# Linear attention and a three-product feed-forward layer on one core: w_phi loaded from ScalarE's queue, the last tile's output in two halves, a new order

## The chip, the core and the metric

The kernel runs on one core of a Trainium2 chip. The core has a matrix engine (TensorE, PE in the profile; its weight loads are shown apart as PEld), a vector engine (VectorE, DVE), a scalar engine (ScalarE, ACT), GpSimd (POOL), and an engine that here only issues transfers (SyncE, SP). Each engine works through its own queue in order and waits there for what the others write. The metric is the device time of one execution in microseconds; lower is better.

## What is computed

q, k and v have 8 batches, 8 heads, 576 tokens and 64 columns. Both stages are in float32.

```
phi(x): p = x @ w_phi (64x128); p -= max|p| per token; [exp(p), exp(-p)]
kv  = phi(k)^T v,  z = sum over tokens of phi(k)
att = (phi(q) kv) / (phi(q) z + 1e-6)          # tokens x 512, all heads side by side
h   = att @ w_in (512x1024);  solu = h * softmax(h)
out = layernorm(solu) * g_ln @ w_out (1024x512)   # 4608 x 512
```

## The kernel before

**Attention.** The work is cut into 16 units, two to a batch. A unit has four heads, handled as two sub-steps ("sub" 0 and 1) of two heads. For each unit SP loads keys in three groups (a group 0 of 512 columns, a small one 1, a group 2 of 512; function `k_load`, L483), values, and queries. TensorE multiplies keys by w_phi (tile `wph`, results `pjk`), VectorE takes the maximum and subtracts it, ScalarE makes both exponentials. The first three units treat their queries in the same way (`q2_load`, L650, and results `pjq`); the later ones transpose them on VectorE and multiply by a split copy of w_phi (`w_hh`, `w_l`).

Each sub-step has one **visit** (`visit`, L580): TensorE multiplies the previous sub-step's query features by its kv matrix (`num`), then builds the present kv matrix (`kvT`), then the denominators (`den`). A visit needs the sums of the key features that GpSimd makes (`z_half`, L570, is the last of them). VectorE evicts the kv matrix, SP writes it to memory (`dk<-kvs`) and reads it back in another layout by four loads (`kvf<-dk`); the next visit needs them. This is called a turn below. The denominators go from ScalarE through VectorE, which takes the reciprocal (`cmr`), to a store by SP (`d<-cmr`) and come back spread over the partitions (`rb<-d`); GpSimd multiplies by them (`divide`, L828, tiles `xa` and `xb`).

**Feed-forward.** The 4608 tokens are 36 tiles of 128, numbered 0 to 35. float32 products are made of three products of split operands (high by high, high by low, low by high). For a tile ScalarE copies the high part of the input (`mxh`), GpSimd makes the low part (`mxl`), TensorE makes `h` in two half steps of 12 products, VectorE and ScalarE make solu (`eu`) and its statistics. Tiles 0 to 32 are turned by VectorE and a way through memory (`du<-ub`, four loads `uTs<-du`), split by ScalarE (`uhs`) and GpSimd (`uls`); tiles 33 to 35 are turned on TensorE (`uT`) and split by ScalarE and VectorE (`uh`, `ul`). Then `moe_o` (L1152) makes the output in two half steps of 12 products of 512 columns in one bank, `moe_oe` (L1162) evicts it on ScalarE with the scale (`os<-o,sc`), `moe_od` (L1166) stores it from SP's queue.

The weights w_in and w_out come as float64 in eight loads of 1 MB (`wraw`) at the start; ScalarE, VectorE and GpSimd turn them into float32 and split them (`win_h`, `win_l`, `w_out_h`, `w_out_l`), beside the first units of attention.

**What sets the order.** Every step is one entry of a list of operations, made by `op(...)` with an engine, a cost, and the steps and buffers that it needs. The table `SEQUENCE` (L50) names the number of every entry; `Plan.order` (L232) walks through it, gives each buffer to the next that asks for it, and each engine gets its steps in that order. So the table fixes the order on every engine, and which of a tag's buffers a step takes: there are three for the large key and query loads (tag `rk`, L42), two banks `mo`, and for the last tiles two banks `tmo` (L47). A load into a buffer waits on SP until the previous contents have been read, and what is queued behind it on SP waits too.

w_phi is loaded twice, into two corners of `wph`, by `phi_load` (L353); VectorE clears the tile first.

Of the kernel before, what the change touches and what calls it, by code (L numbers as in the profile page):

```python
# [50 lines left out]
    88, 99, 0, 3, 2, 136, 126, 132, 102, 7, 89, 90, 100, 103, 198, 104, 199, 127, 107, 95, 108, 91, 101, 96,  # L51
    130, 8, 131, 14, 92, 133, 230, 105, 128, 97, 186, 137, 197, 134, 93, 129, 35, 98, 145, 224, 135, 94, 142,
    138, 106, 148, 9, 109, 149, 143, 139, 144, 118, 140, 234, 146, 150, 41, 10, 15, 187, 114, 11, 141, 151, 119,
    110, 164, 147, 165, 16, 120, 188, 121, 115, 153, 111, 152, 200, 205, 17, 112, 53, 231, 166, 154, 116, 201,
    36, 193, 232, 189, 156, 4, 233, 117, 167, 202, 155, 194, 169, 113, 37, 203, 225, 18, 158, 168, 157, 122,
    204, 190, 195, 28, 295, 38, 196, 6, 42, 226, 39, 12, 191, 228, 13, 170, 192, 235, 227, 171, 229, 172, 240,
    123, 159, 173, 241, 243, 236, 160, 216, 245, 47, 43, 54, 238, 44, 244, 174, 242, 175, 161, 55, 29, 296, 45,
    162, 246, 217, 328, 124, 30, 247, 249, 284, 248, 207, 56, 251, 250, 125, 218, 40, 208, 176, 31, 219, 48,
    209, 32, 177, 178, 179, 210, 49, 163, 252, 180, 212, 46, 237, 213, 254, 50, 214, 253, 255, 215, 51, 211,
    329, 256, 239, 436, 297, 206, 21, 386, 52, 303, 332, 304, 271, 57, 397, 262, 268, 285, 263, 59, 286, 269,  # L60
    333, 60, 58, 220, 633, 437, 330, 291, 273, 61, 264, 287, 270, 22, 331, 292, 272, 298, 221, 257, 438, 293,
    62, 299, 258, 288, 294, 387, 300, 289, 181, 344, 63, 265, 5, 182, 222, 23, 301, 305, 290, 259, 67, 302, 260,
    76, 314, 338, 79, 183, 73, 334, 184, 85, 64, 261, 306, 315, 310, 316, 398, 307, 311, 24, 317, 223, 267, 345,
    266, 346, 68, 19, 33, 65, 274, 20, 308, 275, 276, 309, 34, 335, 278, 277, 347, 279, 439, 349, 339, 348, 336,
    280, 312, 440, 318, 337, 388, 185, 313, 340, 319, 25, 350, 320, 321, 66, 351, 281, 74, 282, 389, 26, 341,
    352, 390, 75, 393, 391, 353, 27, 394, 441, 355, 442, 354, 372, 342, 373, 356, 77, 322, 374, 283, 70, 323,
    468, 358, 366, 1871, 357, 82, 367, 359, 324, 368, 343, 445, 360, 375, 1913, 1872, 443, 69, 395, 1873, 444,
    86, 361, 80, 1914, 446, 362, 377, 447, 550, 469, 614, 81, 405, 392, 1874, 399, 376, 406, 87, 396, 325, 83,
    326, 470, 363, 400, 1875, 448, 327, 369, 401, 511, 1876, 449, 416, 402, 407, 370, 1877, 371, 471, 408, 78,
    1915, 412, 450, 413, 417, 409, 472, 1880, 451, 477, 452, 473, 403, 475, 84, 404, 1916, 474, 410, 1881, 476,  # L70
    501, 551, 418, 478, 479, 453, 422, 1917, 1882, 500, 1883, 378, 552, 853, 1918, 1884, 1885, 379, 512, 1919,
    1892, 364, 411, 71, 1893, 419, 480, 380, 1894, 1886, 1922, 1923, 481, 423, 454, 424, 414, 482, 457, 455, 72,
    381, 458, 555, 553, 483, 1887, 1924, 425, 1895, 554, 484, 459, 1878, 1925, 415, 426, 456, 427, 556, 428,
    1920, 420, 559, 1926, 557, 1888, 1927, 558, 1896, 421, 560, 1897, 365, 429, 1928, 1898, 485, 460, 1901, 461,
    1934, 561, 1929, 486, 582, 1902, 583, 430, 1935, 502, 1903, 462, 382, 463, 520, 1930, 489, 584, 431, 503,
    664, 1904, 507, 519, 504, 505, 1921, 514, 432, 562, 506, 1936, 513, 563, 508, 490, 383, 564, 515, 509, 530,
    433, 516, 491, 1905, 517, 434, 565, 585, 435, 566, 587, 487, 567, 586, 1937, 464, 588, 488, 384, 510, 1906,
    518, 531, 568, 589, 1938, 591, 1931, 696, 590, 532, 1939, 571, 592, 665, 1879, 1940, 536, 572, 385, 1943,
    1932, 593, 1944, 666, 492, 573, 493, 1907, 1945, 1908, 1946, 521, 1947, 494, 697, 1948, 465, 594, 1889, 595,
    569, 615, 522, 596, 570, 698, 526, 523, 537, 524, 667, 538, 525, 597, 1909, 668, 626, 1949, 495, 1933, 533,  # L80
    975, 527, 1890, 625, 528, 466, 529, 496, 1950, 699, 539, 598, 671, 700, 1910, 540, 541, 542, 534, 497, 669,
    627, 673, 670, 498, 1951, 672, 535, 674, 1899, 467, 675, 543, 499, 1941, 574, 1955, 1956, 2018, 599, 1957,
    576, 575, 600, 603, 544, 676, 545, 1958, 677, 577, 778, 678, 2019, 546, 679, 740, 616, 1959, 680, 729, 681,
    547, 628, 617, 1960, 548, 1952, 618, 549, 604, 1961, 619, 620, 621, 601, 644, 622, 2020, 629, 623, 630, 624,
    1964, 1976, 645, 602, 1965, 703, 605, 701, 578, 705, 631, 2021, 810, 682, 632, 646, 702, 704, 706, 1900,
    650, 2022, 1942, 685, 2023, 779, 2024, 606, 683, 2027, 1966, 1967, 1968, 579, 1969, 580, 728, 607, 707,
# [1182 lines left out]
```

## Time and profile before

| | us |
|---|---|
| median of 3 runs | 719.25 (719.08 to 719.99) |
| the profiled execution | 717.91 |
| its span, first to last instruction | 716.1 |
| TensorE busy | 694.4 (97% of the span) |
| GpSimd busy | 513.7 |
| VectorE busy | 483.5 |
| ScalarE busy | 368.7 |

The granted clock of TensorE was 0.997 in the mean. The profile is of one execution, so its times lie within its own 717.91 us, which is 1.34 us less than the median. Matmuls are pipelined, so a row's length is longer than the distance to the next row; distances are taken from the starts. Nearly every row has the line L263, that of the helper through which all instructions go, so rows are told apart by their tiles: `out<-in`.

### The profile page before, as it was taken

The numbers are of one execution on the slowest core, as the hardware profiler recorded it, in microseconds if no ns is written. First come the engines' busy times: TensorE is split into PE (matmuls) and PEld (weight loads), VectorE is DVE, ScalarE is ACT, GpSimd is POOL, SyncE is SP. The second block draws the span as 40 slices with busy tenths as digits, with TensorE's granted clock in tenths as the row PEclk, the third lists the DMA queues.
The fourth block names the chain that finished last, engine by engine and source line by source line (L and its number), as shares of the span: only waits on it lengthen the run. The fifth ranks groups of instructions, "written<-read, shape, count | busy, mean of one in ns | idle before, by whom it ended". The sixth has DMA issues, their size and how long they took to land.

```text
span 716.1 us, 13369 instructions
## 1 busy us (share of the span) xinstructions
PE 694.4 (97%) x4858; PEld 517.8 (72%) x4858; DVE 483.5 (68%) x795; ACT 368.7 (51%) x683; POOL 513.7 (72%) x501
## 2 busy tenths in 40 slices
PE   6999889999999999999999999999999999999997
PEld 5656567777777777777776777777787777788886
DVE  5999878656867678478566688676687574544422
ACT  4888645644753555546555555545544554324221
POOL 1136999996889878887978987986877777445151
PEclk9999999999999999999999999999999999999999
DMA  7784365644763565637357367745664443512331
GB/s 258 286 274 103 79 181 167 189 136 118 199 189 121 159 194 159 199 106 205 111 161 183 118 179 185 192 133 139 177 182 119 144 135 77 155 56 72 125 102 75
DMA packets 113649, 109.96 MB, mean 154 GB/s; under 512 B 57648, under 2 KB 90928, under 8 KB 113072
## 3 DMA queue, kind: packets, MB, share of 16 engines
q1 hardware_dynamic: 113584, 109.11, 52.7%
q8 instruction: 39, 0.64, 0.4%
q14 instruction: 26, 0.21, 0.1%
HBM read 76.68 MB, written 32.39 MB: 152 GB/s over the span
## 4 chain that ended last, share of the span: by engine, by line
PE 81%; DVE 6%; DMA 5%; SPq 2%; ACT 2%; issue 2%; POOL 2%; POOLq 0%; ACTq 0%
PE o L263 26%; PE h L263 24%; PE kvT L263 9%; PE num L263 8%; PE pjk L263 5%; PE den L263 4%; PE pq L263 3%; DVE w L263 2%; SPq L263 2%; DMA kvf<-dk 2%; DVE m L263 1%; DMA dk<-kvs 1%; POOL xa L263 1%; DMA rawk<-in_k 1%; DMA rb<-d 1%
## 5 line engine op out<-in xcount | busy, mean ns | idle before, releaser
L263 ACT ACTIVATE ek<-dk 128x512 f32<-128x512 f32 (+1 forms) x160 | 86.5, 584 | 50.7 <-DVE dk L263 49.0
L263 PE MATMUL o<-w_out_h,uhs 128*128 128x512 f32 x264 | 106.5, 403 | 0.0
L263 PE MATMUL o<-w_out_h,uls 128*128 128x512 f32 x264 | 104.2, 395 | 0.0
L263 PE MATMUL o<-w_out_l,uhs 128*128 128x512 f32 x264 | 104.1, 394 | 0.0
L263 POOL TENSOR_TENSOR uls<-uTs,uhs 128x1024 fp32r<-128x1024 f32 x33 | 79.1, 2396 | 27.6 <-ACT uhs L263 21.1
L263 PE MATMUL h<-win_h,mxh 128*128 128x512 f32 x288 | 93.1, 404 | 0.1
L263 PE MATMUL h<-win_l,mxh 128*128 128x512 f32 x288 | 89.4, 392 | 0.0
L263 PE MATMUL h<-win_h,mxl 128*128 128x512 f32 x288 | 89.4, 391 | 0.0
L263 DVE TENSOR_REDUCE nm<-h 128x1 f32<-128x1024 f32 x36 | 43.8, 1217 | 60.1 <-PE h L263 60.0
L263 POOL TENSOR_TENSOR zt<-ek 128x512 f32<-128x512 f32 x52 | 67.2, 1293 | 16.8 <-ACT ek L263 15.2
L263 POOL TENSOR_TENSOR hq<-rawq,hq 64x1152 fp32r<-64x1152 f32 x26 | 69.0, 2655 | 9.6 <-issue 6.1
L263 PE MATMUL num<-fq,kvf 128*64 128x288 f32 x512 | 69.2, 412 | 2.9 <-DMA kvf<-dk 2.1
L263 ACT ACTIVATE fq<-pT 128x576 f32<-128x576 f32 x104 | 68.1, 678 | 7.4 <-DVE pT L263 7.4
L263 ACT ACTIVATE eu<-h,nm 128x1024 f32<-128x1024 f32 x36 | 40.1, 1115 | 53.2 <-DVE nm L263 47.6
L263 PEld LDWEIGHTS h<-win_l,mxh 128*128 128x128 f32 x288 | 54.0, 188 | 12.1
L263 PEld LDWEIGHTS h<-win_h,mxl 128*128 128x128 f32 x288 | 54.1, 188 | 12.1
L263 DVE TENSOR_TENSOR eu<-h,eu 128x1024 f32<-128x1024 f32 x36 | 43.8, 1217 | 27.4 <-ACT eu L263 27.3
L263 PE MATMUL kvT<-ek,rawv 128*64 128x256 f32 x512 | 61.1, 380 | 0.0
L263 DVE TENSOR_REDUCE m<-pjk 128x4 f32<-128x512 f32 (+1 forms) x80 | 48.4, 621 | 18.3 <-PE pjk L263 18.2
L263 DVE STREAM_TRANSPOSE blk<-pq 128x288 f32<-128x288 f32 x104 | 45.4, 457 | 22.0 <-PE pq L263 17.8
L263 PEld LDWEIGHTS h<-win_h,mxh 128*128 128x128 f32 x288 | 50.8, 189 | 10.9 <-issue 1.4
L263 PEld LDWEIGHTS num<-fq,kvf 128*64 128x64 f32 x512 | 34.5, 136 | 32.7 <-issue 10.2
(107 smaller groups left out, 1444.4 us busy)
## 6 DMA issues: line engine op xcount, KB each, us to landing
du<-ub SPq DMA_DIRECT2D x33, 512.0 KB, 2.8
uTs<-du SPq DMA_DIRECT2D x132, 128.0 KB, 3.4
rawq<-in_q SPq DMA_DIRECT2D x26, 576.0 KB, 4.5
rb<-d SPq DMA_DIRECT2D x64, 144.0 KB, 3.6
out<-os SPq DMA_DIRECT2D x36, 256.0 KB, 3.1
rawk<-in_k SPq DMA_DIRECT2D x32, 256.0 KB, 3.8
rawv<-in_v SPq DMA_DIRECT2D x32, 256.0 KB, 4.0
dk<-kvs SPq DMA_DIRECT2D x28, 192.0 KB, 2.3
```

The lines of the kernel that those rows point to most:

```text
L263: return self.tc.keep_in_program_order(method(*args, **kwargs))
```

## The change

Three things change. `phi_load` issues its two transfers from ScalarE's queue instead of SP's. For tile 35 the output is computed in two halves of 256 columns, each in a bank of its own (the first in a `tmo`, the second in an `mo` bank), all 24 products of a half before the next half; each half is evicted and stored by itself. The table `SEQUENCE` is replaced; its numbers from tile 35 on name other entries as well, since there is one more eviction and one more store.

```diff
@@ SEQUENCE = (
-    88, 99, 0, 3, 2, 136, 126, 132, 102, 7, 89, 90, 100, 103, 198, 104, 199, 127, 107, 95, 108, 91, 101, 96,
...
     def phi_load(j):
-        nc.sync.dma_start(out=wph[j * D : (j + 1) * D, j * F : (j + 1) * F], in_=w_phi)
+        nc.scalar.dma_start(out=wph[j * D : (j + 1) * D, j * F : (j + 1) * F], in_=w_phi)
...
-        op(("wp", j), "sync", dma(4 * D * F, True), -40 + j, phi_load, (j,))
+        op(("wp", j), "scalar", 600, -40 + j, phi_load, (j,))
...
+    LAST = NTOK // P - 1
+
+    def moe_o_last(t, half, tag):
+
+        uh, ul = M["uh", t], M["ul", t]
+        o = M["o", t, half] = bank(tag, [P, DM], "o")
+        cs = slice(half * 256, half * 256 + 256)
+        for fc in range(8):
+            for x, w in ((uh, "h"), (uh, "l"), (ul, "h")):
+                nc.tensor.matmul(
+                    o[:, :256], lhsT=x[:, fc, :], rhs=w_out_part(w, fc)[:, cs],
+                    start=(fc == 0 and x is uh and w == "h"), stop=(fc == 7 and x is ul),
+                )
+
+    def moe_oe_last(t, half):
+        if half == 0:
+            M["os", t] = sb("m2k", [P, DM], name="os")
+        nc.scalar.activation(
+            out=M["os", t][:, half * 256 : half * 256 + 256], in_=M["o", t, half][:, :256], func=AF.Copy, scale=M["sc", t]
+        )
+
+    def moe_od_last(t, half):
+        cs = slice(half * 256, half * 256 + 256)
+        nc.sync.dma_start(out=out[t * P : (t + 1) * P, cs], in_=M["os", t][:, cs])
...
+        for hf in range(2 if t == LAST else 0):
+            tg = ("tmo", "mo")[hf]
+            op(n("o", hf), "tensor", 24 * mm(256), z + 13 + 3 * hf, moe_o_last, (t, hf, tg),
+               [n("ul", i) for i in range(2)] + ([n("o", 0)] if hf else []), [(tg, n("o", hf))], [n("uh"), n("ul"), n("o", hf)])
...
+        if t == LAST:
+            continue
```

The new table keeps the rough order: a step of TensorE moves by about one place in the mean, one of SP by seven. Three places are shown, each before and now.

SP, at the start. `rawk` are keys, `rawq` queries of unit 0 (before, `rawq_108` is its first group, `rawq_110` the second and small one, `rawq_106` the third; now they are `rawq_106`, `rawq_110` and `rawq_147`), `rawv` and `vz` values, `wraw` 1 MB of weights. Before:

```order
L263 DMA rawk<-in_k 128x512
L263 DMA rawk<-in_k 128x128
L263 DMA wph<-in_w_phi 64x128 x2
L263 DMA rawq_106<-in_q 128x512
L263 DMA rawq_108<-in_q 128x512
L263 DMA rawq_110<-in_q 128x128
L263 DMA wraw_114<-in_w_in 128x2048
L263 DMA rawv<-in_v 128x512
L263 DMA vz_74<-in_v 64x128
L263 DMA vz_76<-in_v 64x128 x2
L263 DMA rawk<-in_k 128x512
```

Now, in the same place:

```order
L264 DMA rawk<-in_k 128x128
L264 DMA rawk<-in_k 128x512
L264 DMA rawq_106<-in_q 128x512
L264 DMA rawk<-in_k 128x512
L264 DMA rawq_110<-in_q 128x128
L264 DMA vz_74<-in_v 64x128
L264 DMA wraw_113<-in_w_in 128x2048
L264 DMA rawv<-in_v 128x512
L264 DMA rawk<-in_k 128x128
L264 DMA rawq_147<-in_q 128x512
L264 DMA wraw_151<-in_w_in 128x2048
```

The w_phi loads are gone from SP (they stand first on ScalarE now). Unit 0's third key group is the fourth load instead of the last row shown before, and it takes the third `rk` buffer; its third query group, before ahead of the weights in a buffer of its own, is now behind a 1 MB load and takes the buffer of the first key group.

SP, some 60 to 95 us in, around the load of unit 3's last key group, `rawk_1187` before and `rawk_901` now; `cmr` is the reciprocal denominator that VectorE makes, `d1` its store. Before:

```order
L263 DMA rawq_1104<-in_q 128x1152
L263 DMA kvf_1127<-dk_1102 32x12x32
L263 DMA d1_1174<-cmr_1168 128x9
L263 DMA rawq_1179<-in_q 128x1152
L263 DMA rawk_1183<-in_k 128x512
L263 DMA rawk_1187<-in_k 128x512
L263 DMA vz1_76<-in_v 64x128
L263 DMA rawv_1204<-in_v 128x512
```

Now, around the same load:

```order
L264 DMA d1_886<-cmr_817 128x9
L264 DMA rb_896<-d1_886 64x2x288
L264 DMA rawk_901<-in_k 128x512
L264 DMA rb_896<-d1_886 64x2x288
L264 DMA dk_929<-kvs_924 128x384
L264 DMA d1_980<-cmr_962 128x9
L264 DMA kvf_986<-dk_929 32x12x32 x4
```

The load stood behind the store of unit 2's first denominator (`d1_1174`). It now stands behind that of unit 0's second (`d1_886`), an earlier one, and two further denominator stores, unit 1's second (`d1_980`) and unit 2's first, come after it.

ScalarE, at the end of the program. `os<-o,sc` is an eviction of output, `uhs` and `uh` the high parts of the turned tiles, `eu` the exponentials. Before, tile 33's eviction is the last:

```order
L263 CAST uhs<-uTs 128x1024
L263 ACTIVATE os<-o,sc 128x512
L263 ACTIVATE eu,sm<-h,nm 128x1024
L263 CAST uhs<-uTs 128x1024
L263 ACTIVATE os<-o,sc 128x512
L263 CAST uh<-uT 128x512 x2
L263 ACTIVATE os<-o,sc 128x512 x3
```

Now the last is that of tile 27:

```order
L264 ACTIVATE os<-o,sc 128x256
L264 ACTIVATE os<-o,sc 128x512
L264 CAST uhs<-uTs 128x1024
L264 ACTIVATE eu,sm<-h,nm 128x1024
L264 ACTIVATE os<-o,sc 128x256
L264 ACTIVATE eu,sm<-h,nm 128x1024
L264 ACTIVATE os<-o,sc 128x512
L264 CAST uh<-uT 128x512
L264 CAST uhs<-uTs 128x1024
L264 ACTIVATE os<-o,sc 128x512
L264 CAST uh<-uT 128x512
L264 ACTIVATE os<-o,sc 128x512 x2
```

The second half eviction of tile 35 has eight instructions behind it. The last `uhs`, tile 27's, has moved behind the first `uh` of tile 33. On TensorE the last half step was tile 33's second, behind tile 27's; now it is tile 27's second, behind tile 33's.

On GpSimd the order in the front changes in this: of the eight steps between unit 3's first query split and tile 0's `mxl` (three products with `rb`, three `win_l`, two `w_out_l`) the first was a product with `rb`; now a `w_out_l` stands ahead of it.

4 lines of the change are left out of this document (added), and 272 rows, old and new, of the table SEQUENCE.

## The prediction

> **What bounds the kernel now.** I read the page's busy shares first, then the busy time of each engine by stretches of 40 us, then what TensorE (PE) waited for, then the chain that ended last, and the timeline at both ends.
>
> ```profile
> PE 694.4 (97%) x4858; PEld 517.8 (72%) x4858; DVE 483.5 (68%) x795; ACT 368.7 (51%) x683; POOL 513.7 (72%) x501
> ```
>
> TensorE is busy 694.4 of 716.1 us, so 21.7 us of idle time are all that another order of the same products can give. By stretches (columns: stretch, its length, PE busy, PEld, DVE, ACT, POOL, each with its count, granted clock, DMA share, GB/s):
>
> ```profile
> 0.00:40.00 40.00, 32.91 (x378) 24.15 (x380) 32.15 (x51) 26.56 (x56) 4.95 (x18) 0.96 0.77 262
> 40.00:80.00 40.00, 36.09 (x427) 23.22 (x425) 38.83 (x58) 31.70 (x67) 26.07 (x12) 1.00 0.54 162
> 80.00:120.00 40.00, 35.66 (x240) 26.43 (x238) 31.53 (x47) 22.08 (x45) 38.15 (x30) 1.00 0.58 160
> ...
> 200.00:240.00 40.00, 38.30 (x270) 29.18 (x268) 27.03 (x51) 19.99 (x38) 34.82 (x33) 1.00 0.59 166
> ```
>
> The idle time lies in the first 120 us: 7.09, 3.91 and 4.34 us, 15.3 together. From there to the last product little is left, 1.7 us of it in 200 to 240. In 40 to 80 VectorE is nearly full (38.83 of 40), in 80 to 120 GpSimd is (38.15 of 40). The longer waits of TensorE (total, times, longest):
>
> ```profile
> PE pjk L263 <- DMA wph<-in_w_phi: 4.6, 1, 4.6
> ...
> PE pjk L263 <- DMA rawk<-in_k: 2.1, 1, 2.1
> PE num L263 <- DMA kvf<-dk: 2.1, 3, 1.0
> PE pq L263 <- ACT E L263: 1.8, 1, 1.8
> ```
>
> The chain that ended last shows where the second and the fourth of these lie (start, length, what):
>
> ```profile
> 61.72 5.21 DMA rb<-d
> ...
> 84.44 0.54 PE pq L263 x2
> ...
> 86.76 0.22 DVE cmr L263
> ...
> 88.39 5.54 DMA rawk<-in_k
> ...
> 94.07 1.16 PE pjk L263 x16
> ...
> 102.07 2.09 PE num L263 x16
> ...
> 117.80 2.16 PE num L263 x16
> ```
>
> Unit 3's last key load is issued at 88.39 only because it stands in SP's queue behind the store of a denominator that VectorE finishes at 86.98. TensorE has to wait for it until 94.07. The products at 102.07 and 117.80 (unit 3's two visits) end the front; from there TensorE sets the pace.
>
> **The change, part by part.**
>
> *w_phi on ScalarE's queue.* The start of the timeline (start, length, engine):
>
> ```profile
> 0.84 0.27 DVE L263 MEMSET wph<- 128x256 f32 x1 [0.84 <-PEq L1259]
> ...
> 1.63 1.19 SPq L263 DMA_DIRECT2D wph<-in_w_phi  x2
> ...
> 4.57 3.20 PE L263 MATMUL pjk<-wph,rawk 128*128 128x256 f32 x18 [4.57 <-DMA wph<-in_w_phi]
> ...
> 11.13 2.75 PE L263 MATMUL pjq<-wph,rawq 128*128 128x256 f32 x18 [2.21 <-issue]
> ...
> 11.80 1.79 PEld L263 LDWEIGHTS pjq<-wph,rawq 64*128 64x128 f32 x16 [0.40 <-DVE dk L263]
> ...
> 11.81 1.15 ACT L263 ACTIVATE wraw<-wraw 128x1024 f32<-128x1024 f32 x1 [9.81 <-DMA wraw<-in_w_in]
> ```
>
> The loads can't go out before the memset of their tile ends at 1.11. On SP the first went out at 1.63, behind two key loads; on ScalarE, which has nothing to do until 11.81, it goes out at about 1.15. So everything that waits for w_phi may start 0.48 us earlier, TensorE at 4.09. A trace of a load on ScalarE's queue isn't there: if it lands as fast as on SP the gain is 0.48; if ScalarE's first load starts slowly, nothing or a few tenths lost. The two copies to w_hh and VectorE's difference, which move here too, lie in ScalarE's 9.81 us of idle time and ahead of VectorE's first work.
>
> *The last tile's output.* It has 48 products of 256 columns for 24 of 512. No product of 256 columns in this type is in the trace; the nearest rows are those of 288 columns with a new weight each, and of 512:
>
> ```profile
> 98.78 0.29 PE L263 MATMUL pq<-hq,w_l 128*128 128x288 f32 x1
> 98.91 0.30 PE L263 MATMUL pq<-hq,w_hh 128*128 128x288 f32 x1
> ```
> ```profile
> 711.68 0.39 PE L263 MATMUL o<-w_out_l,uh 128*128 128x512 f32 x1
> 711.91 0.40 PE L263 MATMUL o<-w_out_h,ul 128*128 128x512 f32 x1
> ...
> 712.34 0.69 ACT L263 ACTIVATE os<-o,sc 128x512 f32<-128x512 f32 x1 [2.06 <-PE o L263]
> ```
>
> They start 0.13 and 0.23 us apart. 24 x 0.23 = 5.52 us now; 48 x 0.13 = 6.24 if a product can't follow faster than at 288 columns, 5.52 if it goes by the columns: 0 to +0.7. I take +0.2, near the columns, since 0.13 is itself 288/512 of 0.23. The Trainium skill ("TensorE: Matmul & The Clock Gate", "Back-to-back issue gap") gives 262 cycles for 256 columns and 518 for 512, so no cost at all, but warns there that small products in a stream with weight loads go slower than its formula; the sum by it lies between 0 and the same +0.7.
>
> What the split was to shorten isn't shortened: in the new order tile 35 isn't the last to finish. The last product, eviction and store belong to tile 27, in 512 columns, as those of tile 33 did before. So the end stays as it is: product at 711.91, eviction to 713.03, store, end at 716.1. The two half evictions lie some 25 us and more ahead of that, beside products; a whole one takes 0.69. Tile 27's second input is later than it was: after tile 33's transposes ScalarE makes a copy of it, then GpSimd the difference:
>
> ```profile
> 694.37 1.04 ACT L263 CAST uhs<-uTs 128x1024 fp32r<-128x1024 f32 x1
> ...
> 695.54 2.39 POOL L263 TENSOR_TENSOR uls<-uTs,uhs 128x1024 fp32r<-128x1024 f32 x1 [5.79 <-ACT uhs L263]
> ```
>
> 1.04 + 2.39 and a half copy ahead of them, about 4.1 us with the handovers, stand beside two half tiles of output products, 24 x 0.23 = 5.5. That is 1.4 us of cover: no cost, and at most 1 or 2 us if it fails.
>
> *The new order in the front.* Unit 3's last key load stands on SP ahead of two denominator stores now, where it stood behind them. The wait for it (2.12 us) goes. The other long wait, 1.80 us at 84.44, was for an eviction that ScalarE held back, since the input copy of tile 0 stood ahead of it and waited for GpSimd; the evictions go first now. Both waits are 3.9 us, with the start 4.4. GpSimd doesn't allow all of it:
>
> ```profile
> 67.09 1.42 POOL L263 TENSOR_TENSOR xa<-E,rb 128x576 f32<-128x576 f32 x1 [6.47 <-DMA rb<-d]
> ...
> 76.49 2.50 POOL L263 TENSOR_TENSOR w_out_l<-w,w_out_h 128x512 fp32r<-128x512 f32 x2
> ...
> 99.78 1.30 POOL L263 TENSOR_TENSOR zacc<-zacc,ek 64x512 f32<-64x512 f32 x1
> ```
>
> Its sum for unit 3 is ready at 101.08, 0.99 us ahead of the visit at 102.07. Unless GpSimd comes earlier, the visit gains 1.0 us at most. It does come earlier: a w_out_l step (1.25 us, half of 2.50) is put into its idle time ahead of 67.09, and the denominators that the step at 67.09 waits for (the transfer at 61.72) are no longer behind a later store on SP. The gain on GpSimd is between 0 and its whole idle time of 6.47; I take 1.25 for the step and as much for the earlier start, 2.5. That is the gain of the front: **-2.5 us** (0 to -4.4), the start included, since VectorE and GpSimd set its pace. One thing there is worse: the first unit's third query load takes a buffer that the first key products must free (at about 7.3), where it had one of its own. Two loads of that size behind a 1 MB load in the trace, their issue and their landing (the row of the issues by size, last column us to landing):
>
> ```profile
> 4.92 0.43 SPq L263 DMA_DIRECT2D rawv<-in_v  x1
> ...
> 8.55 0.54 SPq L263 DMA_DIRECT2D rawk<-in_k  x1
> ...
> 12.48 1.01 DVE L263 TENSOR_TENSOR dq<-pjq,m 128x512 f32<-128x512 f32 x2
> ```
> ```profile
> rawk<-in_k SPq DMA_DIRECT2D x1, 256.0 KB, 5.1
> ```
> ```profile
> rawv<-in_v SPq DMA_DIRECT2D x1, 256.0 KB, 7.7
> ```
>
> With 5.1 us it lands at 12.4, and its products start 0.6 late against 11.80; the key products behind them, already loaded, then follow at once, and VectorE has work of this unit until some 13 (13.49 now). I take 5.1, since that load too went out 4 us after the large one, and cost it at nothing inside the 2.5.
>
> *The new order in the middle.* From unit 5's first visit on there is the same set of products between any two visits; only neighbours change places. After a visit, its result goes out and comes back through four loads on SP; in all 28 such turns 136 other transfers stand between, where 156 did. One such transfer holds SP for:
>
> ```profile
> 207.04 0.61 SPq L263 DMA_DIRECT2D uTs<-du  x1
> ```
>
> At the visits with the least cover it is as before or better, but for unit 7's first (9 for 4: five more, 0.5 to 0.6 each, up to +2.5 where no product hides them). The three waits of this kind cost 2.1 us before; I take no change, -1.7 to +2.5.
>
> *Sum.* -2.5 + 0.2 + 0 = -2.3 us. The profiled execution took 717.91 us (span 716.1, 1.8 around it), 1.34 less than the median of 719.25. So 715.6 in its own terms, and **717.0** as a median.
>
> **The rivals.** A measurement of this kernel can tell 0.2% from no change, 1.44 us: faster is below 717.8, slower above 720.7.
>
> *The front is held elsewhere.* VectorE's work is the same and it is full in 40 to 80, so GpSimd may get its inputs no sooner. Then unit 3's first visit gains the 1.0 us of slack alone: -1.0 + 0.2 = -0.8, 718.4, no change. For it: 38.83 of 40. Against it: GpSimd idles 6.47 us in the same stretch.
>
> *All the waits go.* 1.80 + 2.12 + 0.48 at the front, and the 1.7 in the middle: -6.1 + 0.2, 713.3. GpSimd's 38.15 of 40 speaks against it.
>
> *Slower: the buffer that isn't free.* The third query load waits for a buffer, and the next unit's first key load takes the same buffer, so it can go out only when the late products are done. At 7.7 us the first lands at 15.0, 3.2 us late against 11.80; the second comes, I estimate, 1 us after its turn. VectorE has some 1 us to spare in 40 to 80, so nothing of the 4.2 us is caught up: -2.3 + 4.2 = +1.9, 721.2. It decides from 3.7 us on (2.3 + 1.44). For it: a 1 MB load is ahead of it, as of the load that took 7.7. Against it: the load that took 5.1 went out as long after such a one.
>
> **How the numbers follow.** The forecast 0.51, front held elsewhere 0.28, all waits gone 0.08, the late buffer 0.13. Of the forecast's own spread (front 0 to -4.4, split 0 to +0.7, middle -1.7 to +2.5) I put 0.46 below 717.8, 0.04 on no change and 0.01 above. So faster 0.54, no change 0.32, slower 0.14. The range, 713.8 to 721.0, takes in the forecast's spread and the front held elsewhere, and leaves out most of the late buffer and half of all waits gone, about 0.17.
>
> **What would show it.** Right: TensorE's first product at about 4.1; no wait for rawk near 92; unit 3's visits at about 99.5 and 115.3 for 102.07 and 117.80; products of 256 columns 0.12 us apart; the end as now, 4.2 us from the last product's start, with 512 columns. Wrong: the third query products after 14, VectorE idle there; GpSimd's first step of the group at 67.09 no earlier; new waits for kvf, unit 7 above all, of over 2 us; a wait for uls ahead of the last products.

## The result and the profile after

| | before | after |
|---|---|---|
| median of 6 runs each, us | 719.18 | 725.25 |
| lowest and highest | 717.73 to 719.99 | 723.4 to 726.89 |
| the profiled execution | 717.91 | 723.58 |
| its span | 716.1 | 721.8 |

The ratio is 1.0084, with an interval from 1.0063 to 1.0105: the change costs about 6 us, where 2.3 fewer were forecast and 721.0 was the upper end of the range. Of the runs in the table further down, the ratios leave out four executions that took 1156 us (e3), 1771 us (e7), 3293 and 2427 us (before), while the medians shown for e3 and e7 count theirs.

TensorE's row on the page of after:

```profile
PE 699.5 (97%) x4882; PEld 520.9 (72%) x4882; DVE 478.5 (66%) x795; ACT 369.6 (51%) x684; POOL 513.4 (71%) x501
```

It was busy 694.4 us before. So 5.1 of the 5.7 us by which the span grew are *busy* time of TensorE, though the change adds only 24 records, those of the halved products. A list of waits alone can't explain this result.

Next, the span is cut at three points: unit 3's first visit, unit 5's first visit, and the end of the last product. (Columns as in the stretches of 40 us.) Before:

```profile
0.00:102.07 102.07, 87.15 (x914) 61.20 (x916) 88.11 (x130) 70.14 (x147) 52.04 (x46) 0.98 0.62 198
102.07:179.24 77.17, 76.75 (x525) 57.10 (x524) 52.39 (x93) 39.83 (x74) 67.17 (x61) 1.00 0.56 155
179.24:712.31 533.07, 530.53 (x3423) 399.54 (x3422) 342.97 (x572) 258.02 (x461) 394.48 (x396) 1.00 0.51 145
```

After:

```profile
0.00:97.79 97.79, 86.70 (x912) 60.69 (x912) 84.12 (x129) 71.83 (x149) 49.59 (x45) 1.00 0.62 205
97.79:176.82 79.03, 77.79 (x525) 57.37 (x524) 52.66 (x96) 39.99 (x74) 69.86 (x64) 1.00 0.55 154
176.82:717.47 540.65, 535.00 (x3447) 402.82 (x3446) 341.74 (x571) 257.12 (x461) 393.97 (x394) 1.00 0.50 143
```

The front gained 4.28 us up to unit 3's first visit. Of that 1.86 was lost again before unit 5's first visit, which comes at 176.82 for 179.24: 2.42 us early, and 2.5 had been forecast (these are two single executions; how far such a difference can be trusted is said under "Why the prediction was wrong"). All of the loss is in the third stretch, 7.58 us longer; the end adds 0.54 (721.80 - 717.47 for 716.10 - 712.31). In the third stretch TensorE's idle time rose from 2.54 (533.07 - 530.53) to 5.65, by 3.11, and its busy time by 4.47. By tile, the same stretch for the products of `h`, before and then after:

```profile
179.24:712.31 533.07, 176.98 (x721) 132.54 (x720) 75.42 (x62) 37.29 (x62) 1.00 0.51 145
```
```profile
176.82:717.47 540.65, 179.88 (x721) 132.54 (x720) 75.28 (x62) 37.32 (x62) 1.00 0.50 143
```

And for the products `num` of the visits:

```profile
179.24:712.31 533.07, 49.70 (x368) 24.78 (x368) 17.72 (x46) 1.00 0.51 145
```
```profile
176.82:717.47 540.65, 51.24 (x368) 26.01 (x368) 17.68 (x46) 1.00 0.50 143
```

The same 720 products of `h` took 2.90 us more, the same 368 records of `num` 1.54. With the idle time that is 3.11 + 2.90 + 1.54 = 7.55 of the 7.58 us. So there are two things to explain: waits, one of them with a slow stretch behind it, and a slower pace of `h`.

**The wait.** Two of TensorE's waits after (total, times, longest); both lie behind unit 5's first visit:

```profile
PE num L264 <- issue: 2.0, 1, 2.0
PE num L264 <- DMA kvf<-dk: 1.6, 1, 1.6
```

The longer of them on TensorE's timeline, at the visit that follows unit 5's first, and then all engines in three stretches of 3.41 us there (the field behind the five engines is the granted clock):

```profile
195.72 0.40 PE L264 MATMUL o<-w_out_h,uls 128*128 128x512 f32 x1
198.13 3.70 PE L264 MATMUL num<-fq,kvf 128*64 128x288 f32 x16 [2.02 <-issue]
```
```profile
195.19:198.60 3.41, 1.39 (x8) 0.80 (x9) 2.35 (x4) 1.00 (x2) 3.41 (x2) 1.00 0.65 173
198.60:202.01 3.41, 3.41 (x17) 2.12 (x15) 2.63 (x4) 0.64 (x3) 2.41 (x2) 0.50 0.51 187
202.01:205.42 3.41, 3.41 (x46) 2.03 (x42) 0.58 (x1) 1.89 (x3) 1.39 (x1) 1.00 0.66 210
```

TensorE idled 2.02 us, and from 198.60 on the granted clock was 0.50 for 3.41 us: these 16 products took 3.70 us, where those of other visits take 2.16. The 1.54 us of `num` are this. The profile calls the releaser "issue", so the cause must be looked for by hand. The products need the turn of unit 5's first visit: `kvs` stored (`dk`), then four loads `kvf`. SP's timeline before and after:

```profile
184.44 0.34 SPq L263 DMA_DIRECT2D du<-ub  x1
...
187.04 0.32 SPq L263 DMA_DIRECT2D dk<-kvs  x1
188.93 2.62 SPq L263 DMA_DIRECT2D kvf<-dk  x4
```
```profile
183.16 0.34 SPq L264 DMA_DIRECT2D du<-ub  x1
189.11 0.32 SPq L264 DMA_DIRECT2D uTs<-du  x1
189.52 0.38 SPq L264 DMA_DIRECT2D d<-cmr  x1
189.99 0.38 SPq L264 DMA_DIRECT2D dk<-kvs  x1
190.43 0.42 SPq L264 DMA_DIRECT2D uTs<-du  x1
192.28 1.95 SPq L264 DMA_DIRECT2D kvf<-dk  x3
...
195.41 0.56 SPq L264 DMA_DIRECT2D kvf<-dk  x1
```

And what SP waited for from 176 to 200 after, with VectorE's row for `kvs`:

```profile
SPq L264 <- DMA du<-ub: 10.7, 2, 5.5
```
```profile
186.55 0.57 DVE L264 STREAM_TRANSPOSE kvs<-kvT 128x384 f32<-128x384 f32 x1
```

`kvs` was ready at 187.12. But a load of tile 7's `uTs` now stands ahead of its store on SP, and that load waits 5.5 us until tile 7's own store, `du<-ub`, has landed. So `dk` goes out 2.87 us after it could, and the fourth `kvf` at 195.41, behind two more `uTs`. Before, all four were out at 191.55.

**The pace of h.** Seven pairs of `h` products in a row, the first and the last, late in the program, before and after:

```profile
640.13 0.61 PE L263 MATMUL h<-win_h,mxh 128*128 128x512 f32 x2
...
642.85 0.61 PE L263 MATMUL h<-win_h,mxh 128*128 128x512 f32 x2
```
```profile
640.49 0.63 PE L264 MATMUL h<-win_h,mxh 128*128 128x512 f32 x2
...
643.28 0.63 PE L264 MATMUL h<-win_h,mxh 128*128 128x512 f32 x2
```

The six steps take 2.72 us before and 2.79 after, at a full granted clock and with no wait. Over the whole trace a pair starts 0.4587 us after the last one before and 0.4653 after; the products of `o` kept 0.2325 each. No instruction of `h` was changed.

### The profile page after: what moved, and what is told of

Read it like the earlier page. It is cut to its first block, busy times and chain, and to the rows that moved or that the text cites. A ratio compares the mean times of both kernels' runs of the same rounds, so it can differ in the third digit from the quotient of the medians.

```text
span 721.8 us, 13404 instructions
## 1 busy us (share of the span) xinstructions
PE 699.5 (97%) x4882; PEld 520.9 (72%) x4882; DVE 478.5 (66%) x795; ACT 369.6 (51%) x684; POOL 513.4 (71%) x501
## 4 chain that ended last, share of the span: by engine, by line
PE 77%; DMA 5%; DVE 2%; SPq 2%; POOL 2%; issue 1%; ACT 1%; ACTq 0%; POOLq 0%
PE h L264 25%; PE o L264 24%; PE kvT L264 9%; PE num L264 8%; PE pjk L264 4%; PE den L264 3%; PE pq L264 3%; SPq L264 2%; DMA du<-ub 1%; DMA uTs<-du 1%; DMA rawq<-in_q 1%; DMA dk<-kvs 1%; DVE eu L264 1%; DVE nm L264 0%; PE mtp L264 0%
## 5 line engine op out<-in xcount | busy, mean ns | idle before, releaser
L264 PE MATMUL h<-win_h,mxh 128*128 128x512 f32 x288 | 94.7, 410 | 0.0
L264 PE MATMUL num<-fq,kvf 128*64 128x288 f32 x512 | 70.7, 419 | 5.9 <-issue 2.0
L264 ACT CAST uhs<-uTs 128x1024 fp32r<-128x1024 f32 x33 | 34.6, 1048 | 53.9 <-DMA uTs<-du 47.8
```

What stands on the lines that cost most here:

```text
L264: return self.tc.keep_in_program_order(method(*args, **kwargs))
```

## The experiments

Four theories are named in the expectations. **A**: the new order costs, by waits in the turns. **B**: the load on ScalarE's queue slows the products of `h`. **C**: the split does. **A'** came after the first four runs: the new order moves tiles to other addresses, and the pace of `h` depends on these.

The runs, each timed against the kernel before on its chip; the chips differ, so runs are compared by their ratios. "First" is the start of TensorE's first product, "unit 5" that of unit 5's first visit, "middle" the time from there to the start of the last product, "h pair" the mean distance of two pairs of `h`, "o" that of two products of `o` with 512 columns; all are from one profiled execution, in us. In the diffs, the table `SEQUENCE` is written by what it holds (in the files it is a list of numbers), and other lines are left out.

| run | median | ratio to before | first | unit 5 | middle | h pair | o |
|---|---|---|---|---|---|---|---|
| before | 719.18 | | 4.57 | 179.24 | 532.7 | 0.459 | 0.233 |
| after | 725.25 | 1.0084 (1.0063 to 1.0105) | 5.46 | 176.82 | 540.3 | 0.465 | 0.233 |
| e1_order_and_split | 727.59 | 1.0128 (1.0091 to 1.0166) | 4.39 | 177.51 | 545.8 | 0.465 | 0.233 |
| e2_wphi_alone | 720.63 | 1.0026 (0.9997 to 1.0055) | 6.02 | 179.18 | 532.3 | 0.459 | 0.233 |
| e3_split_alone | 719.27 | 1.0007 (0.9986 to 1.0029) | 4.58 | 181.24 | 532.2 | 0.459 | 0.233 |
| e4_order_alone | 727.05 | 1.0117 (1.0087 to 1.0148) | 4.40 | 177.58 | 542.8 | 0.465 | 0.233 |
| e5_aligned | 723.19 | 1.0063 (1.0034 to 1.0092) | 5.39 | 177.74 | 537.6 | 0.461 | 0.232 |
| e6_shifted | 719.01 | 1.0006 (0.9980 to 1.0031) | 4.39 | 177.79 | 534.8 | 0.465 | 0.232 |
| e7_one_turn | 722.74 | 1.0049 (1.0027 to 1.0071) | 5.47 | 176.39 | 538.2 | 0.465 | 0.233 |
| e8_front_only | 716.45 | 0.9965 (0.9949 to 0.9982) | 5.45 | 178.11 | 533.8 | 0.461 | 0.232 |
| e9_to_unit5 | 718.30 | 0.9989 (0.9967 to 1.0010) | 5.45 | 176.45 | 536.3 | 0.459 | 0.233 |
| e10_three_turns | 718.91 | 0.9995 (0.9978 to 1.0012) | 5.79 | 178.05 | 534.1 | 0.459 | 0.233 |
| e11_front_wphi_on_sp | 718.45 | 0.9979 (0.9961 to 0.9998) | 4.59 | 180.04 | 532.7 | 0.461 | 0.232 |
| e12_best | 720.14 | 1.0009 (0.9983 to 1.0035) | 5.43 | 183.59 | 533.5 | 0.459 | 0.233 |
| e13_all_moved_32 | 724.49 | 1.0051 (1.0025 to 1.0077) | 4.40 | 176.95 | 536.0 | 0.466 | 0.233 |
| e14_all_moved_128 | 719.36 | 0.9985 (0.9955 to 1.0016) | 4.63 | 182.90 | 533.3 | 0.465 | 0.230 |
| e15_output_tiles_moved | 717.04 | 0.9975 (0.9952 to 0.9998) | 4.58 | 176.80 | 529.2 | 0.458 | 0.229 |
| e16_front_and_addresses | 713.05 | 0.9920 (0.9899 to 0.9941) | 5.85 | 178.04 | 530.2 | 0.458 | 0.229 |

### The three parts, one by one

**e1_order_and_split**: the change without its first part.

```diff
-        nc.scalar.dma_start(out=wph[j * D : (j + 1) * D, j * F : (j + 1) * F], in_=w_phi)
+        nc.sync.dma_start(out=wph[j * D : (j + 1) * D, j * F : (j + 1) * F], in_=w_phi)
```

> The changed kernel with w_phi's loads back on SP; order and split stay. The trace of the change showed TensorE's first product 0.89 us later, new waits in the middle, and every pair of h products 0.466 us for 0.457. Theory A (all but the late start comes with the order): 725.25 - 0.9 = 724.3 us, first product near 4.6, h pairs still 0.466. Theory B (the loads on ScalarE's queue also slow the h products, 432 pairs x 0.008 = 3.5 us): 720.8 us, h pairs 0.457. Theory C (the split slows them): as A.

**e2_wphi_alone**: the kernel before with that line from `nc.sync` to `nc.scalar`.

```diff
-        nc.sync.dma_start(out=wph[j * D : (j + 1) * D, j * F : (j + 1) * F], in_=w_phi)
+        nc.scalar.dma_start(out=wph[j * D : (j + 1) * D, j * F : (j + 1) * F], in_=w_phi)
```

> The kernel before, with only w_phi's loads moved to ScalarE's queue. Theory A: 719.2 + 0.9 = 720.1 us at most, first product near 5.4, h pairs 0.457 as before; less if VectorE's slack hides a part. Theory B: 719.2 + 0.9 + 3.5 = 723.6 us, h pairs 0.466. What the prediction said: 718.7 us, first product at 4.1.

**e3_split_alone**: the kernel before with tile 35's output in halves (`moe_o_last`, `moe_oe_last`, `moe_od_last` as in the change), in the old order with one more eviction and store in it.

```diff
+        for hf in range(2 if t == LAST else 0):
...
+        if t == LAST:
+            continue
```

> The kernel before, with only tile 35's output in two halves of 256 columns (the eviction of the first half as early as its buffer allows). Theories A and B, and the prediction: 719.2 + 0.2 = 719.4 us, h pairs 0.457. Theory C (the split slows the h products): 722.9 us, h pairs 0.466.

**e4_order_alone**: the kernel before, with its own loads and its own tile 35, in the new order.

```diff
-SEQUENCE = BEFORE
+SEQUENCE = AFTER   # by the steps' names, tile 35 whole
```

> The kernel before, with only the new order (w_phi on SP, tile 35's output whole, its eviction and store where the second half's stood). Theory A: 725.25 - 0.9 - 0.2 = 724.1 us, h pairs 0.466, waits ahead of the visits near 135, 198, 275 and 432. Theories B and C, where the order brings only the waits: 720.7 us, h pairs 0.457. What the prediction said of the order: 2.5 us faster than before, 716.7.

Measured: the order by itself costs 1.17%, and with it come the slow `h` (0.465) and the longer middle, in both kernels that have it. w_phi and the split, each alone, leave `h` at 0.459 and the middle at 532; neither can be told from no change. B and C fall, A stands for the place. That the order can slow products that wait for nothing was not yet explained. In e1 the wait behind unit 5's first visit was longer than in after, 3.22 us, and the slow clock too:

```profile
201.00:202.50 1.50, 1.50 (x10) 0.85 (x8) 0.57 (x1) 0.19 (x1) 1.50 (x1) 0.50 1.06 296
```

### Waits and addresses

The compiled programs give every tile an address in the order of first use. In the new order a small tile (`m4`, 144 bytes a partition) is first used ahead of three of the five tiles that hold the inputs of `h`, the weights that TensorE loads. Before, all five start at 64 bytes past a multiple of 256; after, two do, and three start at 224.

**e5_aligned**: after, with `m4` and `mcol` padded to 192 bytes; of the five, two now start at 64 and three at 0.

```diff
-        st["m4", sub] = sb("m4", [P, 2 * NBLK])
+        st["m4", sub] = sb("m4", [P, 48], name="m4")[:, : 2 * NBLK]
...
-        st["mc", sub] = sb("m4", [P, NM], name="mcol")
+        st["mc", sub] = sb("m4", [P, 48], name="mcol")[:, :NM]
```

> The changed kernel with one more thing: the small m4 and mcol tiles hold 192 bytes a partition instead of 144 (only the first 144 are used). In the new order an m4 tile is the first user of its place ahead of the input tiles of the h products, and its 144 bytes put three of the five at addresses that are not multiples of 64; with 192 all five are. Theory A' (the h products are slower because their weights lie at such addresses): h pairs back from 0.466 to 0.459 us, 432 x 0.007 = 3.0 us, so 725.25 - 3.0 = 722.2 us. Rival (the pace comes with the order itself, with what runs beside the products): 725.2 us, h pairs 0.466.

**e6_shifted**: before, with an unused tile that moves four of the five by 32 bytes, to 96.

```diff
+        if "gap" not in M:
+            M["gap"] = work.tile([P, 8], F32, tag="gap", bufs=1, name="gap")
+            nc.vector.memset(M["gap"], 0.0)
```

> The kernel before, with an unused tile of 32 bytes a partition (and a memset of it on VectorE) ahead of the input tiles of the h products: four of the five no longer lie at multiples of 64. Theory A': h pairs from 0.458 to 0.466 us, 719.2 + 3.0 = 722.2 us, with the old order and its waits. Rival: 719.2 us, h pairs 0.458.

**e7_one_turn**: after, with one turn mended: on SP the store of unit 5's first turn stands ahead of tile 7's first `uTs` load, and its four loads stand together. SP's order there:

```diff
+dk<-kvs
 uTs<-du
 d<-cmr
-dk<-kvs
+kvf<-dk x4
-uTs<-du
-kvf<-dk x3
-uTs<-du x2
-kvf<-dk
+uTs<-du x3
```

> The changed kernel with five entries of SP's queue moved, for one turn (unit 5, first state): its store ahead of the load of tile 7's transposed input that waited 5.5 us for another store, and its four loads one behind the other. Theory A (new waits in the middle, each from its place in SP's queue): the visit at 198.13 comes at once after the products ahead of it, 2.2 us earlier, and the stretch at half clock behind it (1.4 + 0.4 us) goes too: 725.25 - 4.0 = 721.3 us. Rival (the time is lost to the next wait): 724 to 725 us, the wait at 275 longer.

**e8_front_only**: the new order up to unit 3's second visit and the old one behind it, w_phi on ScalarE, tile 35 whole, `m4` padded as in e5.

```diff
-SEQUENCE = AFTER
+SEQUENCE = AFTER[:543] + [s for s in BEFORE if s not in AFTER[:543]]
```

> The new order up to the third unit's second visit (the first 543 steps), the old order of the rest behind it; w_phi on ScalarE's queue, tile 35 whole, the m4 tiles at 192 bytes. By the two traces TensorE lost 18.5 us up to 120 us before (start and excess over the usual pace) and 12.7 after. Theory A (the new order is better in the front, worse in the middle, and slows h by its addresses): 719.2 - 5.8 = 713.4 us, h pairs 0.459. Rival (the front's gain is eaten by what follows whatever the order): 718 to 720 us, new waits between 120 and 280 us.

Measured: e5 brings `h` to 0.461, some two thirds of the way back; its time, 1.0063, isn't apart from that of after. e6 slows `h` to 0.465 in the old order, by nothing but an unused tile and its memset. Its middle is 2.1 us longer, but its front was 1.45 shorter in the profiled run, and its time is no change: for the pace this shows A', for the time not. In e7 the products come at 195.62 without a wait and with a full clock; SP and TensorE there:

```profile
186.72 0.32 SPq L257 DMA_DIRECT2D dk<-kvs  x1
188.41 0.32 SPq L257 DMA_DIRECT2D uTs<-du  x1
...
189.30 2.62 SPq L257 DMA_DIRECT2D kvf<-dk  x4
```
```profile
195.62 2.16 PE L257 MATMUL num<-fq,kvf 128*64 128x288 f32 x16
213.70 1.68 PE L257 MATMUL num<-fq,kvf 128*64 128x288 f32 x12 [1.12 <-DVE bst L257]
```

Its median is 2.5 us below that of after (1.0049 for 1.0084, intervals that just overlap), where the wait and the slow clock were 2.02 + 1.54 = 3.6: the next visit has a wait of 1.12 in their place. e8 is faster than before, by 0.35%. The front's gain is real, and the loss is in the order from unit 3 on: e5, which has the same padding and follows the new order to the end, is at 1.0063.

### How much of the new order is good

**e9_to_unit5**: as e8, cut at step 761 (unit 5's first visit) in place of 543, `m4` at 256 bytes. **e10_three_turns**: after with e7's edit, the four `kvf` loads of the first turns of units 7 and 11 together and earlier in the same way, and `m4` at 256 bytes. **e11_front_wphi_on_sp**: e8 with w_phi on SP, as in e1. **e12_best**: as e9, cut at 535.

```diff
-SEQUENCE = AFTER[:543] + [s for s in BEFORE if s not in AFTER[:543]]
+SEQUENCE = AFTER[:761] + [s for s in BEFORE if s not in AFTER[:761]]   # 535 in e12
...
-        st["m4", sub] = sb("m4", [P, 48], name="m4")[:, : 2 * NBLK]
+        st["m4", sub] = sb("m4", [P, 64], name="m4")[:, : 2 * NBLK]
```

> As e8_front_only, but the new order up to unit 5's first visit (761 steps instead of 543), the old order behind it, and the m4 and mcol tiles at 256 bytes, so that all five input tiles of the h products lie at odd multiples of 64, as they do before. Theory A (up to unit 5's first visit the new order is ahead: 176.82 us after, 179.31 before; behind it, it loses): 719.2 - 2.5 = 716.7 us, or 1.3 less than e8_front_only for the later cut, 715.1 us; h pairs 0.4585 if odd multiples are what counts, 0.461 if multiples of 64 are enough. Rival (what is gained early is lost behind, whatever the order): 719 us.

> The changed kernel with three turns mended on SP (unit 5's first as in e7_one_turn, unit 7's first and unit 11's first with their four loads one behind the other and the large loads behind them) and the m4 tiles at 256 bytes. If the loss is made of these places: 725.25 - 2.5 (measured, e7_one_turn) - 1.6 (the wait at 275) - 1.2 (the wait at 432) - 2.9 (h pairs 0.4653 to 0.4585, 432 of them) = 717.1 us. Rival (the waits move on to the next place): 719.8 us, what e7_one_turn and the addresses give alone.

> As e8_front_only (716.45 us), with w_phi's loads back on SP. Theory A (on ScalarE's queue w_phi lands some 0.9 us later, but SP gets to the third query load earlier, whose products start at 13.0 instead of 14.5): 716.45 + 0.6 = 717.0 us, first product 4.4, third query products near 14.5. Rival (the later start counts): 716.45 - 0.9 = 715.5 us.

> As e8_front_only (716.45 us), with the cut eight steps earlier (535), where the old order has no wait of 1.4 us at the joint, and the m4 tiles at 256 bytes (h pairs 0.459 for 0.461, 0.9 us): 716.45 - 1.4 - 0.9 = 714.2 us. Rival (the joint's wait comes back elsewhere): 715.6 us.

Measured: e9 isn't apart from before. Its unit 5 is 2.8 us early, but where the old order goes on, two waits for inputs of `o` stand at 190.83 and 193.27, 0.98 and 1.71 us, with the low clock behind them, and take that back:

```profile
193.50:195.00 1.50, 1.50 (x5) 1.12 (x5) 0.00 (x0) 1.50 (x4) 1.42 (x2) 0.52 0.49 77
```

e10 comes from 1.0084 to 0.9995, so three turns and the addresses together undo the loss. It isn't ahead of before, though: in the profiled run its front is 1.2 us shorter, and its middle 1.4 longer. e11 against e8 isn't settled (0.9979 to 0.9965, the intervals overlap). e12, meant as the best of all, missed: at 133.67 TensorE had waited 3.3 us for VectorE, and the clock was down behind that:

```profile
PE pq L256 <- DVE dk L256: 3.3, 1, 3.3
```
```profile
135.00:136.50 1.50, 1.50 (x5) 1.12 (x5) 0.11 (x1) 0.00 (x0) 1.50 (x2) 0.50 0.49 114
```

That trace is of one of its slower executions (723.24 us, the median is 720.14). Cut and padding changed together; the cut eight steps earlier seems to cost more than the better padding gave (1.0009, where e8 has 0.9965).

### The addresses by themselves

**e13_all_moved_32** and **e14_all_moved_128**: before, with one unused tile of 32 or 128 bytes ahead of all work tiles.

```diff
+    gap = work.tile([P, 8], F32, tag="gap", bufs=1, name="gap")    # [P, 32] in e14
+    nc.gpsimd.memset(gap, 0.0)
```

> The kernel before, with an unused tile of 32 bytes a partition ahead of all working tiles, so that none of them lies at a multiple of 64 any more. If such addresses cost time: h pairs at 0.465 for 0.458 (2.9 us), and whatever the other weights lose; 719.2 + 2.9 = 722.1 us at least, and from unit 5's first visit to the last product at least 535.0 us for 532.7. Rival (the pace of a product changes, the time doesn't): 719.2 us.

> The control of e13: the same with 128 bytes, so that every working tile keeps its place within 128. Both theories: 719.2 us, h pairs 0.458, 532.7 us from unit 5's first visit to the last product. If it comes out like e13, it is the extra tile and not the addresses.

**e15_output_tiles_moved**: before, with an unused 128-byte tile ahead of the first `big` and of the first `m2k` tile, so that the weights of `o` (`uhs`, `uls`) start at 64 where seven of eight started at 192, and those of `h` stay at 64. **e16_front_and_addresses**: e8 without its padding, with these two tiles and one that sets off the first `m4`, so that all of them start at 64.

```diff
+    gaps = {}
+
     def sb(tag, shape, dtype=F32, name=None):
-        return work.tile(shape, dtype, tag=place(tag), bufs=1, name=name or tag)
+        if tag in ("big", "m2k") and tag not in gaps:
+            gaps[tag] = work.tile([P, 32], F32, tag="gap_" + tag, bufs=1, name="gap_" + tag)
+        x = work.tile(shape, dtype, tag=place(tag), bufs=1, name=name or tag)
+        if tag == "m4" and tag not in gaps:                 # e16 alone
+            gaps[tag] = work.tile([P, 24], F32, tag="gap_m4", bufs=1, name="gap_m4")
+        return x
```

> The kernel before, with two unused tiles of 128 bytes, one ahead of the eight tiles that hold the weights of the output products (seven of them go from 192 to 64 modulo 256) and one ahead of the input tiles of the h products, which so keep 64 modulo 256. If the address decides the pace: h pairs 0.4585 as before, output products 0.2296 for 0.2324, 864 x 0.0028 = 2.4 us, so 719.2 - 2.4 = 716.8 us and 530.3 us from unit 5's first visit to the last product (before 532.7). Rival (the address doesn't decide): 719.2 us.

> e8_front_only (the new order up to unit 3's second visit, the old order behind it, 716.45 us) with the weights of the h and of the output products all at 64 modulo 256: h pairs 0.459 for 0.461 (0.9 us), output products 0.2296 for 0.2324 (2.4 us): 716.45 - 3.3 = 713.2 us. Rival (the front's gain was that run's luck): 716.8 us, as e15.

Measured: e13 moves `h` to 96 and `o` to 224: both are slower (0.466, 0.2334), and the time is up by 0.51%, on the same instructions in the same order but for one memset. e14 was meant as a control and isn't one: it puts `h` at 192 (slower, 0.465) and `o` at 64 (faster, 0.2296), and the two cancel, with no change in time. From it came the rule that e15 and e16 use on purpose. e15 is 0.25% faster than before, with an interval that ends just short of no change (0.9998); e16, with the good front, 0.80%: 713.05 us, the fastest of all, some 12 us below after. The output products of the last half step, before and in e16:

```profile
709.34 0.40 PE L263 MATMUL o<-w_out_h,uh 128*128 128x512 f32 x1
...
711.91 0.40 PE L263 MATMUL o<-w_out_h,ul 128*128 128x512 f32 x1
```
```profile
705.73 0.39 PE L256 MATMUL o<-w_out_h,uh 128*128 128x512 f32 x1
...
708.23 0.39 PE L256 MATMUL o<-w_out_h,ul 128*128 128x512 f32 x1
```

Eleven steps take 2.57 us before and 2.50 in e16.

## Why the prediction was wrong

**The front, -2.5: right, though the profiled pair alone would not show it.** Unit 5's visit is 2.42 us early in that pair. Part of this may be luck: the profiled execution of before had 3.41 us at half clock, from 11.61 on, and that of after had none from 10.87 on, where its record of the clock begins, to this visit. Over all traces, unit 3's first visit comes at 99.7 to 105.5 in the seven with the old order up to there and at 96.8 to 99.6 in the eleven with the new one. Unit 5's comes at 176.80 to 182.90, 179.2 in the mean, in the same seven, and at 176.39 to 178.05, 177.2 in the mean, in the seven that follow the new order up to it. The times agree: e16 differs from e15 by the new front and w_phi's queue (the weights start at 64 in both), and it is 0.55% faster, 4.0 us, with intervals that lie apart. The wait for rawk is gone, GpSimd's sum for unit 3, at 99.78 before, starts at 96.76, and unit 3's visits come at 97.79 and 113.55, 1.7 earlier than forecast. 1.05 of that went in a new wait at 134.88, for `eu`.

```profile
96.76 1.30 POOL L264 TENSOR_TENSOR zacc<-zacc,ek 64x512 f32<-64x512 f32 x1
```
```profile
134.88 2.16 PE L264 MATMUL num<-fq,kvf 128*64 128x288 f32 x16 [1.05 <-DVE eu L264]
```

**w_phi on ScalarE's queue, -0.48 with "nothing or a few tenths lost" as the other end: wrong in its sign.** The loads go out at 1.14, as forecast, but land later, so TensorE begins at 5.46 and not at 4.09, 0.89 later than before. After, and the same rows of before (size, us to landing):

```profile
1.14 1.19 ACTq L264 DMA_DIRECT2D wph<-in_w_phi  x2
```
```profile
wph<-in_w_phi ACTq DMA_DIRECT2D x2, 32.0 KB, 3.5
```
```profile
wph<-in_w_phi SPq DMA_DIRECT2D x2, 32.0 KB, 2.4
```

SP sends its larger key loads at the same moments. The Trainium skill ("DMA: Bandwidth & Descriptors", "Issuing engines are not separate DMA queues") says that transfers of different engines interleave on the same 16 DMA engines, so that a second issuer saves issue time alone; the 3.5 for 2.4 is in line with that, though no run here separates it from other causes. It cost the sum little: e2 doesn't tell it from nothing.

**The rival of the late buffer** did not decide in after: the third query products start at 13.08 (12.4 forecast; after 14 was to be the sign). The delay that it feared is real in the new order with w_phi on SP: there they start at 14.49 (e1), 14.59 (e4) and 15.30 (e11), though the load goes out earlier than in after (8.20, 8.05 and 8.03 for 8.70). So what was late there was the landing, 6.3 to 7.3 us after the issue, and not the buffer.

```profile
14.59 1.83 PE L256 MATMUL pjq<-wph,rawq 64*128 64x128 f32 x13 [2.87 <-DMA rawq<-in_q]
```

**The split, +0.2: right.** 24 products of 256 columns start 0.12 us apart, so 48 take 5.7 for 5.5; tile 27 is last, in 512 columns, and no wait for `uls` came up. From the last product's start to the end it is 4.7, 0.5 more than forecast.

```profile
688.73 0.28 PE L264 MATMUL o<-w_out_h,ul 128*128 128x256 f32 x1
688.85 0.28 PE L264 MATMUL o<-w_out_h,uh 128*128 128x256 f32 x1
```

**"The new order in the middle", "I take no change, -1.7 to +2.5": the step that failed.** It measured +7.6, in two parts.

First, it counted the transfers between a turn's store and its loads (136 for 156) and gave each the half microsecond for which it holds SP. It did not ask whether a transfer has to wait itself, and it counted only from the store on: the `uTs` load that waited 5.5 us stands ahead of the store. A `uTs` load waits for its own store to land, and with it whatever stands behind it. The turn that the prediction named, unit 7's first, did wait, 1.57 us; the dear one, unit 5's, held three transfers, fewer than the mean of about five, but it had held none before, so the "as before or better" of the prediction does not hold for it. And the price of a wait was put at its length: behind this one the lower clock came near to doubling it, 2.02 + 1.54. That this place in the queue was the cause e7 shows, which moved the store ahead of that load and put the four loads together, and has no wait there; how much each of the two moves gave was not tested. e10 shows what the turns and the addresses are worth together.

Second, "the same set of products" was taken to need the same time. 2.90 us came from their pace, a term that the sum doesn't have. That addresses alone change the pace is shown by e6, e13, e14 and e15, which keep the order of before; that the new order's addresses did it here, by e5, where moving them brings two thirds of it back, and by e10, which has them all at 64 and a pair at 0.459.

## What to carry to other kernels

A place in a DMA queue costs what the entries ahead of it wait, more than how many they are: in a new order, look for a load that reads back what a store in the same queue has just sent, and for what is queued behind it. When the busy time of an engine changes with the same instructions, compare the distance of equal products in streams without waits, and then the addresses of the tiles; a new order can move these. Keep a good part of an order by itself before dropping it: the front of this one, with the addresses set on purpose, beat both kernels.

## What the runs showed of the hardware

**The pace of float32 products goes by where the weights lie.** By the start address of the tile that TensorE loads as weights, modulo 256 bytes: products of `o` with 512 columns start 0.2287 to 0.2296 us apart at 64 (e14, e15, e16), 0.2325 at 192 (seven of eight tiles, before), 0.2334 at 224 (e13). Within one kernel it is the same. In after, a pair of `h` products takes 0.4604 in half steps whose two weight tiles both lie at 64, 0.4653 where one lies at 224 and 0.4669 where both do (27, 196 and 85 pairs); in e8, 0.4590 with both at 64, 0.4592 with both at 0, 0.4623 with one at each (49, 107 and 156 pairs); with both at 96, 0.4659 (e13). A mix of 0 and 64 is slower than either alone, so it isn't only the address of the one tile that counts. The other operand lay at 64 in all runs. So it stays open whether the address itself counts, its place beside the other operand's or beside that of the weights before it, and other addresses were not tried. That is 1 to 2% of such a product.

**A short idle time of TensorE can cost about as much again, and the traces show when.** A wait of 2.02 us (after) was followed by 3.41 us at a granted clock of 0.50, and one of 2.12 us in before, of which the prediction has the row at 94.07, was not. Nor was one of 1.57:

```profile
276.96 2.16 PE L264 MATMUL num<-fq,kvf 128*64 128x288 f32 x16 [1.57 <-DMA kvf<-dk]
```

In all 18 traces, from where the profile has the clock (some 8 to 18 us in), the stretches at 0.50 last 3.41 us or twice that, but for those that the end of the program cuts off. Where a trace has several, their starts lie whole multiples of 3.413 us apart (12.07, 53.03 and 87.17 in e14: 12 and 10 of them). So each span can be cut into windows of that length, laid from the start of a low stretch. After a window at full clock in which TensorE idled 1.81 us or more, the next was at 0.50: 20 windows out of 20. After one with 1.74 us or less, it was at full clock, always. The wait of 2.02 us lies in one window, the first of the three shown above under "The wait". The one of 2.12 us lies across a boundary, at 93.53, with 1.59 us of idle time in the first window:

```profile
90.12:93.53 3.41, 1.82 (x11) 1.28 (x9) 2.08 (x4) 1.31 (x4) 3.25 (x3) 1.00 1.02 364
93.53:96.95 3.42, 2.88 (x25) 2.55 (x26) 2.91 (x4) 0.65 (x3) 3.34 (x5) 1.00 0.47 95
```

So does one of 2.30 us in e14 (218.92 to 221.22, boundary at 220.28, no low clock). Where the windows lie differs from one execution to the next, so whether a wait of about 2 us costs its length or nearly twice that is chance.

The Trainium skill ("TensorE: Matmul & The Clock Gate", "Why this matters for your kernels") warns of idle gaps over about 3 us. These runs differ: waits of 1.81 (e14, at 84.92) and 2.02 us were enough, where they fell into one window. Its Part 1 has the clock set by windows of about 3.4 us that run on by themselves, and by that the same gap could fall either way; the traces agree, with the 3.41 us above.

**What stays open**: the time of w_phi's load by itself (-0.03 to +0.55% in e2; in the new order ScalarE's queue looks the better one, 1.0084 in after against 1.0128 in e1 and 0.9965 in e8 against 0.9979 in e11, with intervals that overlap); why the fronts of one order differ by up to 6 us from one execution to the next. With the old order unit 5's first visit came at 176.80 in e15 and at 182.90 in e14. Stretches at half clock may be a part of it: from 10 us on e15 had none ahead of that visit, and e14 three.
